# Attention with a gated block behind it: first queries loaded beside the first keys, mixing weights loaded later, and one matmul for the rows that two heads share

## The chip, the cores and the metric

The kernel runs on one core of one Trainium2 chip. The metric is the device time of one execution in microseconds (us), as the median of several runs. A core has TensorE (PE, with weight loads shown apart as PEld), VectorE (DVE), ScalarE (ACT), GpSimd (POOL) and SyncE (SP), which here issues every DMA from one queue.

## The reference

32 heads of attention (4 batches of 8 heads) with 1152 keys of 64 numbers, whose 1152 queries are first averaged in pairs to 576. The 8 heads of a batch are put side by side (512 numbers a row) and go through a gated block with a residual:

```python
q_pool = q.reshape(B, H, S // 2, 2, D).mean(axis=3)       # 576 rows
scores = scale * np.matmul(q_pool, k.transpose(0, 1, 3, 2))
attn = np.exp(scores - np.max(scores, axis=-1, keepdims=True))
attn = attn / (np.sum(attn, axis=-1, keepdims=True) + 1e-09)
x = np.matmul(attn, v)                                    # heads side by side: (4, 576, 512)
h = gelu(x @ w_in)                                        # 1024 wide
u, v = h[..., :512], h[..., 512:]
v_n = layer_norm(v) * g_ln
v_s = np.einsum('ts,bsd->btd', w_sg, v_n) + b_sg[None, :, None]   # the mixing weights w_sg
out = x + (u * v_s) @ w_out
```

## The kernel before, in words

**Work.** The heads go in 16 pairs. Numbers are split in a high and a low 16-bit half so that 16-bit matmuls lose nothing that matters. For a pair, `load` fetches keys (`kr`), queries (`qr`, and the last 128 query rows of each head in `qe`) and values (`vr`, or `va` for two pairs that keep their exponentials in 32 bits). `prepare` finds a scale (a square-sum on ACT, line 393; a matmul with ones, L396; three small DVE operations, L400 to L405), adds the query pairs on POOL (`qs`, L423 and L425), splits keys (ACT L428, DVE L431) and queries (ACT L441, DVE L445) and turns them with DMA transposes into `k1` (L435) and `q1` (L449); L438 copies the high halves of the keys into `k2`, whose other rows are zeroed by POOL once (L905, L906).

**Row maxima.** `maxima` multiplies nine blocks of 128 query rows with the keys (L499) and takes the largest entry of each row by a DVE reduction (L505). Of a head's 576 pooled rows, 512 make four blocks; the last 64 rows of both heads share the ninth block. In the kernel before, these shared rows stand in `q1` twice, as block 4 with only head 0's rows filled and as block 5 with only head 1's, and the maxima of the shared block are two matmuls that add up in one bank. DVE makes the block maxima one number a row (`nm`, L529), POOL splits it and writes it beside the queries (`n2`, L535 to L537), and a transpose (L540) makes `q2`, so that the second of two score matmuls subtracts the maximum.

**Attention.** `unit_of` takes 128 keys at a time: two score matmuls (L574) into a bank `s`, the exponential on ACT (L582), its high half on ACT (L588), its low half by subtraction (L593) and the matmuls with the values (L602; L609 for the two 32-bit pairs) into `avp`. `KEEP` says for which share of the units the exponential stays in the bank and DVE subtracts; for the others it goes to memory and POOL subtracts. At a head's end ACT copies `avp` out (L641), DVE inverts the sums (L644, L645), POOL scales (L648).

**Gated block.** `project` and `gmlp` run once a batch, their matmuls (L757, L857) put between those of the next batch's heads; the last batch has none after it. `weights` loads and splits `w_in` and `w_out`; `spatial` loads `w_sg` (L1058, L1061), finds its scale (L1070 to L1083), turns it on PE (L1110, L1112) and splits it (ACT L1121, DVE L1125). Nothing of `weights` starts before `spatial` is done ("sgdone").

**Order.** Every operation is added to a planner, `Schedule`, with an engine, a cost, what it reads and writes, and a due time. The planner fixes the order on each engine; `PASSES` and the table `MOVES` shift due times before the last pass. Each engine and the SP queue then run in that fixed order and wait in place. L920 adds 40 matmuls with ones that only keep PE busy at the start.

Of the kernel before, what the change touches and what calls it, by code (L numbers as in the profile page):

```python
# [222 lines left out]
def attention_gmlp_kernel(  # L223
# [57 lines left out]
    q2 = tiles(const, 2, [128, 10, 128], F16, "q2")  # L281
    mp = tiles(const, 2, [128, 9, 3], F32, "mp")
    qs = const.tile([128, 10, D], F32, name="qs")
    n1 = const.tile([128, 10, 2, D], F16, name="n1")
    n2 = const.tile([128, 10, 128], F16, name="n2")
# [87 lines left out]
    def scales(p, i, due):  # L373
# [36 lines left out]
        add("DVE", 0.64, power, r=[f"ps{p}{i}"], w=[st, f"pm{i}"], due=due, rel=[("x", "sc", p, i)])  # L410

    def prepare(p):
# [5 lines left out]
        for h in range(2):  # L418
            blk = slice(5 * h, 5 * h + 5)

            def pool(h=h):

                nc.gpsimd.tensor_tensor(out=qs[:, 6 * h:6 * h + 4, :], in0=qr[:, h, :, 0, :], in1=qr[:, h, :, 1, :], op=ALU.add)  # L423
                r = slice(64 * h, 64 * h + 64)
                nc.gpsimd.tensor_tensor(out=qs[r, 4 + h, :], in0=qe[r, 0, :], in1=qe[r, 1, :], op=ALU.add)  # L425
# [14 lines left out]
            def q_hi(blk=blk):  # L440
                nc.scalar.activation(out=n1[:, blk], in_=qs[:, blk].rearrange("p (i t) d -> p i t d", t=1).to_broadcast(  # L441
                    [128, 5, 2, D]), func=AF.Copy, scale=s[:, 1:2])
# [5 lines left out]
            def q_turn(blk=blk):  # L448
                nc.sync.dma_start_transpose(out=q1[c][:, blk], in_=n1[:, blk].rearrange("p i t d -> p (i t d)"))  # L449

            add("POOL", 0.97, pool, r=["qr"], w=[f"qs{h}"], due=t + lead("PL", p) + h)
            add("ACT", 0.72, q_hi, r=[f"qs{h}", sct], w=[f"n1{h}"], due=t + lead("QH", p) + h * HS[p > 0])
            add("SP", 0.7, q_turn, late=LATE[1] * (p > 0), issue=1.25, r=[f"n1{h}"], w=[f"q1{c}{h}"], due=t + lead("QH", p) + h * HS[p > 0])
# [4 lines left out]
            add("DVE", 0.46, q_lo, port=True, r=[f"qs{h}", sct, f"n1{h}"], w=[f"n2q{h}"], due=t + lead("QL", p) + h * HS[p > 0])  # L458
# [22 lines left out]
    def maxima(p):  # L481
# [5 lines left out]
        def rows(r):  # L487

            return ([(0, 4), (1, 5)], [0, 1]) if r == 4 else ([(0, r)], [0]) if r < 4 else ([(1, r + 1)], [1])

        def piece_of(group, j0, nj, g):
            nonlocal n
            r0, x = group[0][0], ("x", p, group[0][0], g)
            w = 128 * nj

            def piece():
                for i, (_, ops, _) in enumerate(group):
                    for k, (h, o) in enumerate(ops):
                        nc.tensor.matmul(out=bank(x)[:, w * i:w * i + w], lhsT=q1[c][:, o, :],  # L499
                                         rhs=k1[c][:, h, j0:j0 + nj, :].rearrange("p j k -> p (j k)"), start=(k == 0),  # L500
                                         stop=(k == len(ops) - 1))

            def top():
# [6 lines left out]
            cols = w * sum(len(ops) for _, ops, _ in group)  # L510
            heads = sorted({h for _, _, hs in group for h in hs})
            add("PE", cols / 2400.0 + 0.003 * len(group), piece, r=[f"q1{c}{h}" for h in heads] + [f"k1{c}{h}" for h in heads], w=[x],
                due=due, acq=(x, where))
            add("DVE", w * len(group) / 960.0 + 0.07, top, r=[x], w=[f"mp{c}{a}{g}" for a, _, _ in group], due=due - 0.5, rel=[x])

        for r in range(9):
            ops, hs = rows(r)

            for g in range(2):
                piece_of([(r, ops, hs)], 4 * g, 4, g)  # L520
            if r in (3, 4, 8):
                piece_of([(a, *rows(a)) for a in {3: range(4), 4: (4,), 8: range(5, 9)}[r]], 8, 1, 2)
            if r in (4, 8):
                due = t + lead("X", p) + lead("XS", p) * n * 1.29 if p else -20 + n
                h = r // 8
                nm = nmx[h]

                def done(h=h, nm=nm):
# [725 lines left out]
```

## Time and profile before

| | before |
|---|---|
| median of 3 runs | 638.8 us (638.28 to 639.22) |
| the profiled execution | 635.98 us, of which its span is 634.2 us |
| PE busy | 603.6 us, 95% of the span |
| DVE, ACT, POOL busy | 528.5, 531.0, 380.8 us |
| DMA packets' time on the SP queue | 51.7% of 16 engines' span |

The profiled execution is 2.8 us below the median. The span runs from the first instruction to the last. Busy times of matmuls overlap, since a matmul's record lasts longer than the distance to the next one.

### The profile page before, as it was taken

The numbers are of one execution on the slowest core, as the hardware profiler recorded it, in microseconds if no ns is written. First come the engines' busy times: TensorE is split into PE (matmuls) and PEld (weight loads), VectorE is DVE, ScalarE is ACT, GpSimd is POOL, SyncE is SP. The second block draws the span as 40 slices with busy tenths as digits, with TensorE's granted clock in tenths as the row PEclk, the third lists the DMA queues.
The fourth block names the chain that finished last, engine by engine and source line by source line (L and its number), as shares of the span: only waits on it lengthen the run. The fifth ranks groups of instructions, "written<-read, shape, count | busy, mean of one in ns | idle before, by whom it ended". The sixth has DMA issues, their size and how long they took to land.

```text
span 634.2 us, 18243 instructions
## 1 busy us (share of the span) xinstructions
PE 603.6 (95%) x7228; PEld 409.2 (65%) x7228; DVE 528.5 (83%) x1052; ACT 531.0 (84%) x987; POOL 380.8 (60%) x481
## 2 busy tenths in 40 slices
PE   5899899997999899999999999999999999999997
PEld 3387567864567566667566775676666775776755
DVE  4989899898989999999987999879998997753662
ACT  7478898799999989999999999798999988784420
POOL 8133375477556688855574677785475565962163
PEclk9999999999999999999999999999999999999999
DMA  9988961957655245568678334807772221141002
GB/s 262 236 209 217 185 135 39 198 121 121 129 115 121 61 79 133 111 136 177 114 160 181 35 51 94 154 24 193 132 170 52 68 41 20 12 84 36 26 1 74
DMA packets 129078, 71.49 MB, mean 113 GB/s; under 512 B 107424, under 2 KB 111520, under 8 KB 128864
## 3 DMA queue, kind: packets, MB, share of 16 engines
q1 hardware_dynamic: 128992, 70.33, 51.7%
q8 instruction: 56, 0.92, 0.6%
q14 instruction: 30, 0.25, 0.1%
HBM read 36.23 MB, written 4.72 MB: 65 GB/s over the span
## 4 chain that ended last, share of the span: by engine, by line
PE 64%; DVE 14%; ACT 5%; issue 1%; DMA 1%; POOL 0%; ACTq 0%; DVEq 0%; POOLq 0%
PE px L757 18%; PE s L574 14%; PE avp L602 13%; PE pm L757 7%; PE px L499 7%; DVE mp L505 5%; DVE f L593 2%; PE s L757 1%; ACT f L588 1%; PE avp L609 1%; ACT e L582 1%; DMA x<-in_moe_w_out_dram 1%; DVE n L445 1%; PE pm L857 1%; DVE dn L644 1%
## 5 line engine op out<-in xcount | busy, mean ns | idle before, releaser
L593 POOL TENSOR_TENSOR f<-e,f 128x512 f16<-128x512 f32 (+2 forms) x182 | 193.0, 1068 | 108.1 <-ACT f L588 93.0
L574 PE MATMUL s<-q,k 128*128 128x512 f16 (+1 forms) x1152 | 231.2, 286 | 12.8 <-ACT e L582 5.2
L505 DVE TENSOR_REDUCE mp<-px 128x1 f32<-128x512 f32 (+2 forms) x316 | 199.8, 663 | 18.1 <-PE px L499 16.2
L602 PEld LDWEIGHTS <-f 128*128 128x128 f16 x3780 | 150.4, 97 | 56.3 <-issue 10.6
L602 PE MATMUL avp<-va,f 128*128 128x65 f16 x3780 | 166.0, 193 | 1.5 <-POOL f L593 1.0
L582 ACT ACTIVATE e<-s 128x512 f32<-128x512 f32 (+2 forms) x226 | 124.9, 558 | 15.6 <-PE s L574 11.1
L499 PE MATMUL px<-k,q 128*128 128x512 f16 (+1 forms) x454 | 118.7, 325 | 2.1 <-DVE mp L505 1.6
L574 PEld LDWEIGHTS <-k 128*128 128x128 f16 x1152 | 82.6, 99 | 51.0 <-issue 15.6
L588 ACT ACTIVATE f<-e 128x512 f16<-128x512 f32 (+2 forms) x182 | 107.1, 591 | 4.5 <-issue 2.0
L593 DVE TENSOR_TENSOR f<-s,f 128x512 f16<-128x512 f32 x126 | 85.9, 682 | 22.7 <-ACT f L588 22.3
L582 ACT ACTIVATE s<-s 128x512 f32<-128x512 f32 x126 | 76.9, 611 | 8.1 <-PE s L574 7.5
L588 ACT ACTIVATE f<-s 128x512 f16<-128x512 f32 x126 | 77.4, 614 | 4.3 <-PE avp L602 2.4
L499 PEld LDWEIGHTS <-q 128*128 128x128 f16 x480 | 42.2, 99 | 27.0 <-issue 6.2
L609 PEld LDWEIGHTS avp<-va,e 128*128 128x128 f32 x360 | 46.1, 192 | 3.1
L609 PE MATMUL avp<-va,e 128*128 128x65 f32 x360 | 45.6, 270 | 0.0
L757 PE MATMUL px<-wsg,vz 128*128 128x512 f16 x168 | 43.6, 379 | 0.0
L423 POOL TENSOR_TENSOR qs<-qr 128x256 f32<-128x256 f32 x32 | 25.1, 786 | 22.3 <-DVE n L445 11.2
L757 PE MATMUL px<-wout_h,xg 128*128 128x512 f32 x100 | 38.2, 425 | 0.0
L757 PEld LDWEIGHTS <-win_h 128*128 128x128 f16 x320 | 30.0, 98 | 12.6 <-issue 1.0
L648 POOL TENSOR_TENSOR x<-a,dn 128x320 f32<-128x320 f32 x32 | 25.3, 789 | 17.2 <-DVE dn L645 13.2
L757 PE MATMUL px<-xt,win_h 128*128 128x288 f16 (+2 forms) x220 | 34.9, 262 | 0.0
L757 PEld LDWEIGHTS <-vz 128*128 128x128 f16 x224 | 20.5, 98 | 20.6 <-issue 0.4
(166 smaller groups left out, 1012.3 us busy)
## 6 DMA issues: line engine op xcount, KB each, us to landing
kr<-in_k_dram SPq DMA_DIRECT2D x16, 576.0 KB, 4.6
qr<-in_q_dram SPq DMA_DIRECT2D x16, 512.0 KB, 4.0
vr<-in_v_dram SPq DMA_DIRECT2D x14, 576.0 KB, 4.1
k<-k SPq DMA_DIRECT2D x32, 144.0 KB, 3.1
x<-in_moe_w_in_dram SPq DMA_DIRECT2D x8, 512.0 KB, 5.9
out_dram<-t SPq DMA_DIRECT2D x16, 256.0 KB, 2.3
x<-in_moe_w_out_dram SPq DMA_DIRECT2D x8, 256.0 KB, 3.5
u<-in_moe_w_sg_dram SPq DMA_DIRECT2D x1, 1152.0 KB, 7.0
```

What stands on the lines that cost most here:

```text
L423: nc.gpsimd.tensor_tensor(out=qs[:, 6 * h:6 * h + 4, :], in0=qr[:, h, :, 0, :], in1=qr[:, h, :, 1, :], op=ALU.add)
L445: nc.vector.scalar_tensor_tensor(out=n2[:, blk, 0:D], in0=qs[:, blk], scalar=s[:, 1:2], in1=n1[:, blk, 0, :], op0=ALU.mult, op1=ALU.subtract)
L499: nc.tensor.matmul(out=bank(x)[:, w * i:w * i + w], lhsT=q1[c][:, o, :], rhs=k1[c][:, h, j0:j0 + nj, :].rearrange("p j k -> p (j k)"), sta ...
L505: nc.vector.tensor_reduce(out=mp[c][:, r0:r0 + len(group), g], in_=src, axis=AX.X, op=ALU.max)
L574: nc.tensor.matmul(out=buf(("s", u))[:, col:col + w], lhsT=kk[c][:, hh, j, :], rhs=qq[:, o:o + w], start=(i == 0 and m == 0), stop=(i == 1 ...
L582: nc.scalar.activation(out=s if kept else buf(("e", u))[:, 0:n], in_=s, func=AF.Exp, scale=SCALE * 2.0**-ASH)
L588: nc.scalar.activation(out=buf(("f", u))[:, 0, 0:n], in_=exponentials(), func=AF.Copy)
L593: eng.tensor_tensor(out=f[:, 1, 0:n], in0=exponentials(), in1=f[:, 0, 0:n], op=ALU.subtract)
L602: nc.tensor.matmul(out=avp[:, o:o + m], lhsT=w[:, col:col + 128], rhs=vv, start=(j == 0 and k == 0 and not tail and x == 0), stop=(j == KJ ...
L609: nc.tensor.matmul(out=avp[:, o:o + D + 1], lhsT=e[:, col:col + 128], rhs=vw[c][:, KJ * hh + j, :], start=(j == 0 and k == 0 and not tail) ...
L648: nc.gpsimd.tensor_tensor(out=xbuf[b % 2][:, :, col], in0=a[:, :, 0:D], in1=d.rearrange("p (i o) -> p i o", o=1).to_broadcast([128, 5, D]) ...
L757: nc.tensor.matmul(out=bank(m)[:, o[0] if o else slice(0, cols)], lhsT=l, rhs=r, start=(k + j == 0), stop=(k + j == n - 1), skip_group_che ...
```

## The change

- The load of the first pair's queries is put right behind that of its keys (`D_LQ`); the load of the mixing weights may not start before the planner's 13 us (`R_S`, 0.16 before), and their turning on PE now waits for their scale.
- The zero rows of the first `k2` are written by DVE; POOL zeroes one block of `n1` where it zeroed all of `qs`.
- The shared rows stand in `n1` once, as block 4 with both heads' rows; POOL copies them crosswise into block 9 (`q_cross`: head 0's rows in the first half of the columns, head 1's in the second). Two copies on the SP queue put the high halves of both heads' keys under each other in `kx`, which there is one of (`k_cross`). The maxima of the shared rows are then one matmul where there were two, with the high halves of the keys alone. They are finished with the second head's rows, so that the first `nm` needs four blocks and not five.
- `KEEP` goes from 0.5 to 0.53. In the last batch the first three units of `project` keep off the score banks, and the others wait for the last head's rows; all units of `project` wait for the scales of `w_in`.
- `PASSES`, `MOVES` (69 entries for 76) and several of the planner's costs are other ones, so the order differs on every engine.

```diff
-    q2 = tiles(const, 2, [128, 10, 128], F16, "q2")
+    q2 = tiles(const, 2, [128, 9, 128], F16, "q2")
+    kx = const.tile([128, KJ, 128], F16, name="kx")
...
+            def q_cross():
+
+                for a in range(2):
+                    r = slice(64 * a, 64 * a + 64)
+                    nc.gpsimd.tensor_copy(n1[r, 9, a, :], n1[r, 4, a, :])
+
+            def k_cross(h=h):
+                nc.sync.dma_start(out=kx[64 * h:64 * h + 64], in_=k1[c][0:64, h])
...
+            if h:
+                add("POOL", 0.45, q_cross, r=["n11"], w=["n1x"], due=t + lead("QH", p) + h * HS[p > 0])
...
+            add("SP", 0.41, k_cross, late=LATE[1] * (p > 0), r=[f"k1{c}{h}"], w=[f"kx{h}"], due=t + lead("KC", p) + h * HS[p > 0])
...
-            return ([(0, 4), (1, 5)], [0, 1]) if r == 4 else ([(0, r)], [0]) if r < 4 else ([(1, r + 1)], [1])
+            if r == 4:
+                return q1[c][:, 9, :], kx, [f"q1{c}1", "kx0", "kx1"]
+            return q1[c][:, r, :], k1[c][:, r // 4 if r < 4 else 1], [f"q1{c}{r // 5}", f"k1{c}{r // 5}"]
...
-        add("POOL", 0.57, lambda: nc.gpsimd.memset(qs, 0.0), w=["qs0", "qs1"], due=-99)
+        add("POOL", 0.2, lambda: nc.gpsimd.memset(n1[:, 9], 0.0), w=["n1x"], due=-99)
...
-        add("POOL", 4.0, lambda: zero_k2(0, nc.gpsimd), w=["k2z0"], due=-15, start=R_Z)
+        add("DVE", 2.3, lambda: zero_k2(0, nc.vector), w=["k2z0"], due=-90)
...
-            add("PE", 0.46, turn, r=["sraw", "srawt", "ident"], w=[x], due=dd, acq=(x, ["X", "M"]))
+            add("PE", 0.46, turn, r=["sraw", "srawt", "ident", "wsc"], w=[x], due=dd, acq=(x, ["X", "M"]))
...
-KEEP = (0.5, 0.5)
+KEEP = (0.53, 0.53)
...
-R_K, R_Q, R_V, R_S, R_Z = 0.0, 21.94, (11.42, 9.34), 0.16, 0.0
+R_K, R_Q, R_V, R_S, R_Z = 0.0, 21.94, (11.42, 9.34), 13.0, 0.0
```

On the SP queue the program begins, before the change, with these DMAs (`u`, `x_89` and `graw` are the mixing weights and their bias and gain; `q_77` and `k_73` are the first pair's `q1` and `k1`, `k_75` its `k2`):

```order
L338 DMA kr<-in_k_dram 128x2x576
L1058 DMA u<-in_moe_w_sg_dram 128x2304
L1061 DMA x_89<-in_moe_w_sg_dram 64x576
L1062 DMA x_89<-in_moe_b_sg_dram 128x576
L1063 DMA graw<-in_moe_g_ln_dram 128x4x1
L341 DMA qr<-in_q_dram 128x2x512
L344 DMA qe<-in_q_dram 64x128 x2
L348 DMA vr<-in_v_dram 128x2x576
L435 DMA_TRANSPOSE k_73<-kn 128x9x128
L352 DMA va_86<-in_v_dram 128x9x64 x2
L449 DMA_TRANSPOSE q_77<-n_84 128x5x128
```

With the change the same place reads (lines are those of the changed kernel: L342 and L345 load queries, L460 turns them, L446 turns keys, L436 makes `kx`, L553 makes `q2`):

```order
L339 DMA kr<-in_k_dram 128x2x576
L342 DMA qr<-in_q_dram 128x2x512
L345 DMA qe<-in_q_dram 64x128 x2
L460 DMA_TRANSPOSE q_77<-n_85 128x4x128
L446 DMA_TRANSPOSE k_73<-kn 128x9x128 x2
L460 DMA_TRANSPOSE q_77<-n_85 128x6x128
L1076 DMA u<-in_moe_w_sg_dram 128x2304
L1079 DMA x_90<-in_moe_w_sg_dram 64x576
L1080 DMA x_90<-in_moe_b_sg_dram 128x576
L1081 DMA graw<-in_moe_g_ln_dram 128x4x1
L349 DMA vr<-in_v_dram 128x2x576
L339 DMA kr<-in_k_dram 128x2x576
```

The queries moved ahead of five loads, all four transposes of the first pair ahead of the mixing weights and of the values. Behind these rows stand the two copies into `kx`, two loads of values and one copy into `k2`, and then the first transpose into `q2`.

On DVE, from the first row maximum on, the order before is 12 reductions (L505) and three small operations up to the first `nm`; the rows at the end of that stretch and behind it are:

```order
L505 TENSOR_REDUCE mp0_81<-px2_145 128x1
L505 TENSOR_REDUCE mp0_81<-px1_144 128x1
L400 TENSOR_SCALAR pm0_105<-pm0_146 128x1
L402 TENSOR_SCALAR sc1_108<-pm0_105 128x1
L405 TENSOR_SCALAR sc1_108<-pm0_105 128x1
L529 TENSOR_REDUCE nm0_115<-mp0_81 128x5
```

With the change (reductions are L520, `nm` is L542) 10 reductions and nothing else stand ahead of it:

```order
L520 TENSOR_REDUCE mp0_82<-px2_146 128x4
L520 TENSOR_REDUCE mp0_82<-pm0_147 128x1
L542 TENSOR_REDUCE nm0_116<-mp0_82 128x4
L520 TENSOR_REDUCE mp0_82<-px0_144 128x1
L520 TENSOR_REDUCE mp0_82<-px2_146 128x1
L520 TENSOR_REDUCE mp0_82<-px1_145 128x1
```

The first `nm` moved forward by two reductions and three small operations. The eleven DVE operations on the mixing weights (five small ones for the scale, six of L1125) stood ahead of the first reduction; now the scale's come six rows behind `nm` and the six others between and behind the last reductions of the pair.

## Rows read from the trace of the kernel before

**Rows 1.** The page's busy time of each engine (share of the span, instructions).

```profile
PE 603.6 (95%) x7228; PEld 409.2 (65%) x7228; DVE 528.5 (83%) x1052; ACT 531.0 (84%) x987; POOL 380.8 (60%) x481
```

**Rows 2.** Five stages: window, length, busy PE, PEld, DVE, ACT, POOL, clock, DMA.

```profile
0.00:20.00 20.00, 11.44 (x59) 6.62 (x60) 10.48 (x28) 15.39 (x24) 13.33 (x23) 1.00 0.95 259
20.00:100.00 80.00, 73.55 (x767) 52.70 (x766) 74.19 (x151) 62.18 (x121) 36.04 (x53) 1.00 0.86 186
100.00:400.00 300.00, 289.14 (x3709) 195.74 (x3708) 276.15 (x554) 284.27 (x536) 197.24 (x251) 1.00 0.56 116
400.00:580.00 180.00, 179.39 (x2368) 120.73 (x2367) 141.26 (x273) 156.59 (x294) 115.79 (x140) 1.00 0.39 81
580.00:634.20 54.20, 50.13 (x332) 33.46 (x330) 26.41 (x50) 12.58 (x14) 18.44 (x17) 1.00 0.13 40
```

**Rows 3.** Timeline of the start: start, length, engine, what, [idle time before].

```profile
4.69 1.16 ACT L393 ACTIVATE kn<-kr 128x1152 bf16<-128x1152 f32 x1 [2.18 <-DMA kr<-in_k_dram]
...
8.26 2.12 ACT L1070 ACTIVATE vz<-u 128x2304 bf16<-128x2304 f32 x1 [0.19 <-DMA u<-in_moe_w_sg_dram]
...
9.62 2.01 POOL L906 MEMSET k<- 3x2304 f16 x1
...
12.04 0.73 POOL L423 TENSOR_TENSOR qs<-qr 128x256 f32<-128x256 f32 x1 [0.42 <-DMA qr<-in_q_dram]
...
13.08 0.83 ACT L441 ACTIVATE n<-qs,sc 128x640 f16<-128x640 f32 x1 [0.17 <-POOL qs L425]
...
15.76 2.06 DVE L1125 SCALAR_TENSOR_TENSOR wsg<-px,wsc,wsg 128x512 f16<-128x512 f32 x3
...
18.36 0.59 PE L499 MATMUL px<-k,q 128*128 128x512 f16 x2
```

**Rows 4.** Timeline from the first maxima to the first scores.

```profile
18.99 1.28 DVE L505 TENSOR_REDUCE mp<-px 128x1 f32<-128x512 f32 x2
...
26.14 0.16 DVE L529 TENSOR_REDUCE nm<-mp 128x5 f32<-128x15 f32 x1
...
27.32 1.21 SPq L540 DMA_TRANSPOSE q<-n  x1
...
27.76 1.24 PE L920 MATMUL avp<-unit_b 128*128 128x512 bf16 x5
...
30.85 0.59 PE L574 MATMUL s<-q,k 128*128 128x512 f16 x2 [0.33 <-POOL qs L423]
```

**Rows 5.** Row maxima by form (count, busy us, mean ns), and one timeline row.

```profile
L499 PE MATMUL px<-k,q 128*128 128x512 f16 x302 | 104.0, 379 | 1.7 <-DVE mp L505 1.3 <-DMA q<-n 0.2
L499 PE MATMUL px<-k,q 128*128 128x128 f16 x152 | 15.5, 219 | 0.4 <-DVE mp L505 0.3
L505 DVE TENSOR_REDUCE mp<-px 128x1 f32<-128x512 f32 x271 | 177.0, 680 | 17.1 <-PE px L499 15.4 <-PE px L396 0.6
21.58 0.38 PE L499 MATMUL px<-k,q 128*128 128x128 f16 x4
```

**Rows 6.** POOL's low halves and two of its small operations, by form.

```profile
L593 POOL TENSOR_TENSOR f<-e,f 128x512 f16<-128x512 f32 x126 | 150.2, 1193 | 88.9 <-ACT f L588 75.9 <-PE s L574 3.3 <-PE px L499 3.2
L425 POOL TENSOR_TENSOR qs<-qe 64x64 f32<-64x64 f32 x32 | 11.4, 357 | 1.3
L536 POOL CAST n<-nm 128x5 f16<-128x5 f32 x32 | 7.6, 239 | 2.2
```

**Rows 7.** DMA issues (count, KB each, median us from issue to landing).

```profile
k<-k SPq DMA_DIRECT2D x32, 144.0 KB, 3.1
k<-kn SPq DMA_TRANSPOSE x32, 4.4
```

**Rows 8.** Timeline: the last values' matmuls, the first result of the last block.

```profile
578.36 0.53 PE L602 MATMUL avp<-va,f 128*128 128x65 f16 x12
...
587.74 0.69 ACT L710 ACTIVATE vz<-s,xs 128x512 f32<-128x512 f32 x1 [6.16 <-PE s L757]
```

**Rows 9.** What PE waited for: total us, times, longest.

```profile
PE s L574 <- ACT e L582: 5.2, 12, 1.2
...
PE s L574 <- DMA q<-n: 2.5, 1, 2.5
```

More of the change, by code (lines that the diff above doesn't have):

```diff
@@ L409, in scales @@
         add("PE", 0.04, spread, r=[f"am{c}{i}", "unit"], w=[f"ps{p}{i}"], due=due, acq=(("x", "sc", p, i), ["X", "M"]))
-        add("DVE", 0.64, power, r=[f"ps{p}{i}"], w=[st, f"pm{i}"], due=due, rel=[("x", "sc", p, i)])
+        add("DVE", 0.26 if i else 0.39, power, r=[f"ps{p}{i}"], w=[st, f"pm{i}"], due=due, rel=[("x", "sc", p, i)])
     def prepare(p):
@@ L509, in piece_of @@
             where = (["X", "M", "S"] if r0 < 4 else ["X", "M"]) if p == 0 else ["X", "M"] if p < NP else XB
[L510 to L514, printed above, removed]
+            cols = w * len(group)
@@ L516, in maxima @@
+            add("PE", cols / 2400.0 + 0.003 * len(group), piece, r=sorted({a for r in group for a in rows(r)[2]}), w=[x], due=due,
+                acq=(x, where))
+            add("DVE", w * len(group) / 960.0 + 0.07, top, r=[x], w=[f"mp{c}{a}{g}" for a in group], due=due - 0.5, rel=[x])
         for r in range(9):
-            ops, hs = rows(r)
             for g in range(2):
-                piece_of([(r, ops, hs)], 4 * g, 4, g)
+                piece_of([r], 4 * g, 4, g)
             if r in (3, 4, 8):
-                piece_of([(a, *rows(a)) for a in {3: range(4), 4: (4,), 8: range(5, 9)}[r]], 8, 1, 2)
@@ L535, in split @@
                     nc.gpsimd.tensor_scalar(out=nm, in0=nm, scalar1=1.0 / MW, scalar2=None, op0=ALU.mult)
                     nc.gpsimd.tensor_copy(hi, nm)
-                    nc.gpsimd.tensor_tensor(out=n2[:, 5 * h:5 * h + 5, D + 1], in0=nm, in1=hi, op=ALU.subtract)
-                def turn(h=h):
-                    nc.sync.dma_start_transpose(out=q2[c][:, 5 * h:5 * h + 5, :], in_=n2[:, 5 * h:5 * h + 5, :].rearrange("p i c -> p (i c)"))
-                add("DVE", 0.17, done, r=[f"mp{c}{a}{g}" for a in range(4 * h, 4 * h + 5) for g in range(3)], w=[f"nm{h}"], due=due - 0.5)
+                    nc.gpsimd.tensor_tensor(out=n2[:, blk, D + 1], in0=nm, in1=hi, op=ALU.subtract)
@@ L543, in maxima, with turn @@
+                def turn(blk=blk):
+                    nc.sync.dma_start_transpose(out=q2[c][:, blk, :], in_=n2[:, blk, :].rearrange("p i c -> p (i c)"))
+                add("DVE", 0.17, done, r=[f"mp{c}{a}{g}" for a in range(blk.start, blk.stop) for g in range(3)], w=[f"nm{h}"], due=due - 0.5)
                 add("POOL", 0.76, split, r=[], w=[f"nm{h}", f"n2m{h}"], due=due - 0.5)
-                add("SP", 0.7, turn, late=LATE[2] * (p > 0), issue=1.25, r=[f"n2q{h}", f"n2m{h}"], w=[f"q2{c}{h}"], due=due - 1)
+                add("SP", 0.7 if h else 0.6, turn, late=LATE[2] * (p > 0), issue=1.25, r=[f"n2q{h}", f"n2m{h}"], w=[f"q2{c}{h}"], due=due - 1)
@@ L696, in project @@
             add("SP", 1.1, x_turn, late=LATE[1] * (b < B - 1), issue=1.3, r=[f"xn{ct % 2}"], w=[f"xt{ct}"], due=dc)
-        ready = [f"xt{ct}" for ct in range(CT if b < B - 1 else CT - 1)]
+        last = b == B - 1
+        ready = ["wn0", "wn1"] + [f"xt{ct}" for ct in range(CT - last)]
+        early = ready + (["nm0", "nm1"] if last else [])
+        if last:
+            ready = ready + [f"x{b % 2}{H - 1}"]
         for i in range(5):
```

67 lines of the change are left out of this document (35 added, 32 removed), and 15 rows, old and new, of the table MOVES.

## The prediction

> **What bounds the kernel now.** I read the page first. PE is busy for 95% of the span; DVE, ACT and POOL have 83%, 84% and 60% [rows 1]. The shares alone do not say that PE is the limit, because a matmul's record lasts longer than the distance to the next matmul. So I read the distance: five matmuls of 512 columns in a row take 1.24 us [rows 4], the record of one is 0.38 us [rows 5], so they start (1.24 - 0.38) / 4 = 0.215 us apart. That is the true price of such a matmul in a full queue.
>
> Then I cut the span into stages [rows 2]. Up to 20 us nothing is full. From 20 to 100 us PE has 73.6 of 80 us and DVE 74.2: both matter. From 100 to 400 us PE has 289 of 300, ACT 284, DVE 276: three engines are near their end together. From 400 us on PE has 179.4 of 180 and then 50 of 54, and the others have room. PE's longest named waits are small: 5.2 us in 12 pieces on the exponentials, and one of 2.5 us on a transpose [rows 9]. So a matmul taken away after 400 us should be worth its full price, one before that a part of it.
>
> The start is a chain of its own [rows 3]. ACT begins on the keys at 4.69 us, when they land. The queries are queued behind the mixing weights, and POOL begins to add them when they land, at 12.04; ACT rounds them at 13.08, a transpose follows, and the first row maxima run at 18.36. From there [rows 4] the reductions begin at 18.99, the first `nm` is made at 26.14, its transpose goes out at 27.32 once POOL has split it, and the score matmuls that need it run at 30.85.
>
> **The change part by part.** *Shared rows.* Per pair there were twice two matmuls of 512 columns and two of 128; half of them go: two of 512 and one of 128. Four of 128 columns take 0.38 us, one record 0.219 [rows 5], so they are (0.38 - 0.219) / 3 = 0.054 us apart. A pair saves 2 x 0.215 + 0.054 = 0.48 us, 16 pairs 7.7 us. The reductions stay as they are: one bank is read for the shared rows before and after. Bounds: 7.7 us if PE is the limit everywhere; if it is so only outside 100 to 400 us, and the 16 pairs lie evenly over the 500 us in which maxima run, 300 / 500 x 7.7 = 4.6 of it are lost and 3.1 left. I take 7.7, and come back to the rest as a rival.
>
> *Queries first.* Mixing weights of 1152 KB landed between 4.69 (keys) and 8.26 us [rows 3], an estimate of 320 KB a us. 576 KB of queries directly behind the keys are then there at 4.69 + 1.8 = 6.5 us. POOL must be free by then: its zeroing of both `k2` ends at 9.62 + 2.01 = 11.6 us, and half of that, two operations of 2.01, goes to DVE, so POOL is free at about 7.6. It adds the first head's queries in 0.73 us (8.3) and ACT rounds them in 0.83 (9.1). A transpose takes SP 1.2 us to issue [rows 4], so the queries go out at 9.1, the keys of head 0 at 10.3. The first maxima need both landed: 10.3 plus between 3.1 (the row of a plain copy) and 4.4 us (a keys' transpose) [rows 7] is 13.4 to 14.7. I take 14.2, 4.2 us ahead of 18.36. DVE gets the zeroing: POOL's price for it was 4.0 us; DVE cannot begin on the keys before ACT has squared them at 4.69 + 1.16 = 5.85 us, and is idle for half of the first 20 us [rows 2], so I cost it nothing; without that cover it would be at most 4 us, on the chain.
>
> *First `nm` from four blocks.* It waits for 10 reductions instead of 12 and three small operations. Two reductions end 1.28 us after the first began and one lasts 0.68 [rows 4, 5], so they are 0.60 apart: 6.0 us instead of 26.14 - 18.99 = 7.15, a gain of 1.1. But on SP 13 DMAs now stand between the last transpose of the pair and the first into `q2`: at 0.5 to 0.6 us each they end at about 14.5 + 8 = 22.5, when `nm` is split at about 22. So I count 0.3 of the 1.1 and put the score matmuls at about 26.3 instead of 30.85: the start is worth 4.5 us. Bounds: 2 us if both of its transposes and the SP queue come a microsecond late, 6 if the SP queue never is.
>
> *What the start costs later.* The mixing weights' turning on PE and splitting on DVE and ACT were done before 18.4 us beside idle engines; now they lie among the maxima. On PE they replace matmuls with ones. On DVE they are six operations (three took 2.06 us [rows 3]) and five small ones, near 5 us, in a stage where DVE is 93% busy [rows 2]. Between nothing and the whole 4.5 us can be lost; I take 2.0, since the splitting of `w_in` in the same stage can wait.
>
> *Low halves.* `KEEP` moves 8 of 252 units from POOL to DVE. On DVE I price one like a reduction over as many numbers, 0.60 us, 4.8 us in all; POOL loses 8 x 1.19 = 9.5 [rows 6]. POOL gets 32 copies of 64 x 64, of which a row of this kernel shows neighbours only: a POOL operation on 128 x 5 at 0.24 us and one on 64 x 64 with two inputs at 0.36. I take 0.3, 9.6 us, about what it loses, on an engine that is idle for 40%; hidden. DVE's 4.8 us fall mostly where it is 92% busy: between nothing and 4.8, I take 2.0.
>
> *Copies into `kx`.* 32 DMAs of the kind `k<-k`, 3.1 us from issue to landing [rows 7], about 0.55 us of SP each. In the order the matmuls on `kx` stand late among a pair's 27, so the landing is covered by the other blocks. Zero, with a rival below.
>
> *The end.* From the last values' matmuls at 578.4 us to the first `vz` at 587.7 [rows 8], while the last head's rows are made, PE works on the last batch's first parts and on the batch before. In the new order about as much of both is left for that place. Zero.
>
> Sum against the profiled execution: 635.98 - 7.7 - 4.5 + 2.0 + 2.0 = 627.8 us. The median of the runs lies 2.8 us above that execution, so 630.6, and I say **630.5 us**.
>
> **Rivals.** *ACT and DVE carry the middle.* From 100 to 400 us ACT is at 95% and does the same work as before; DVE does more. Then the matmuls saved there turn into PE idle time: 4.6 us of the 7.7 are lost, 635.1. For it: the three shares in that stage. Against it: ACT has 180 - 156.6 = 23 us of room from 400 to 580, and the order is a new one, so work can move there. The Trainium skill, page Perfetto Trace Analysis, section Identifying the Most-Contended Engine, says that matmul busy time is a poor measure of PE's headroom and that weight-load busy share and FLOPs should be used; here that share is 65% against ACT's 84%, so by that rule ACT would be the engine to relieve and this rival would hold, at 635.1. The trace agrees that records overlap, and says with the distance of 0.215 us that the queue was nevertheless full after 400 us.
>
> *The start does not pay.* If VectorE is the limit from 20 to 100 us, the 4.5 us are given back in full: 633.1. For it: 74.2 of 80 us. Against it: a good part of that is work that is not due before the first gated block.
>
> *Slower: the new waits.* `kx` is one buffer for two pairs in flight, its copies wait on SP for transposes that landed, and all DMAs behind them wait too; POOL waits in place for ACT before its crosswise copies, with low halves behind it. At 8.3 / 16 = 0.52 us of PE wait a pair the gain is gone; at 0.8, a quarter of one copy's landing, the time is 630.5 + 12.8 = 643. For it: SP's and POOL's queues run in fixed order. Against it: PE waited on a transpose once in the whole run, for 2.5 us [rows 9], and POOL has 40% idle time.
>
> **How the numbers follow.** Forecast 0.55 (its own range 626 to 635), middle carried by others 0.20, start without pay 0.10, slower 0.10, and 0.05 for an order that packs better than 626. A measurement here tells 0.2%, 1.3 us. Faster by more: all of the first, third and last case and three quarters of the second, 0.85; within it 0.06; slower 0.09. The range from 623 to 638 leaves out most of the slower case and the far side of the last.
>
> **What would show it.** First maxima near 14 us and first score matmuls near 26; the maxima's matmuls down by 48; PE still above 97% from 400 us; no wait of PE on `kx` of more than 1 us. The forecast is wrong if PE shows new idle time between 100 and 400 us, if the first head's end is not earlier, or if a wait on SP's queue reaches PE.

## The result, and the profile after

The changed kernel takes 645.99 us (median of 4 runs, 643.54 to 648.64), the kernel before 638.65 (its three runs and one more). The ratio of the runs is 1.0133 with a 95% interval of 1.0105 to 1.0162, so the change makes it slower: by 8.5 us by the ratio, which is used from here on, and by 7.3 us by the two medians alone (1.0115, inside the interval). 630.5 was forecast. In what follows one per cent of the kernel before is 6.4 us, and kernels are compared by their ratio to it.

The page of the profiled execution (647.11 us, span 645.3), its busy times and its clock in 40 slices, against [rows 1]:

```profile
PE 601.7 (93%) x7180; PEld 407.5 (63%) x7180; DVE 534.1 (83%) x1062; ACT 530.6 (82%) x987; POOL 374.4 (58%) x487
...
PEclk9999999999799999999999999999999999999999
```

48 matmuls are gone, as the change says, and the share of every engine but VectorE has gone down: work was taken away and waiting came in. One slice also has a lower granted clock. The stages of [rows 2] (window, length, busy PE, PEld, DVE, ACT, POOL, clock, DMA):

```profile
0.00:20.00 20.00, 11.19 (x38) 4.59 (x39) 13.24 (x27) 5.62 (x8) 9.28 (x22) 0.91 0.62 169
20.00:100.00 80.00, 72.11 (x764) 53.53 (x763) 72.23 (x150) 69.46 (x133) 34.22 (x52) 1.00 1.01 222
100.00:400.00 300.00, 282.00 (x3490) 190.40 (x3488) 263.71 (x532) 267.71 (x504) 193.19 (x245) 0.99 0.54 116
400.00:580.00 180.00, 175.13 (x2399) 118.11 (x2398) 155.92 (x301) 168.21 (x319) 114.77 (x147) 1.00 0.45 96
580.00:645.30 65.30, 61.25 (x500) 40.90 (x498) 29.02 (x56) 19.56 (x28) 22.89 (x22) 1.00 0.12 38
```

From 100 to 400 us all four engines do less than before: 282 against 289 us on PE, 264 against 276 on VectorE, 268 against 284 on ACT, 193 against 197 on POOL. Neither ACT nor VectorE became the bound there.

The last stage is longer by 11 us only because everything before it ends later. The copies of `avp` on ACT (L641, in the changed kernel L655) mark the heads' ends. The eighth head, the last of the first batch, ends at 157.3 us (155.1 before) and the last one at 590.4 (578.9); from there on 54.9 us remain, before 55.3. So the larger part of the loss arises after the first batch and before the last head's end. The two profiled executions are 11.1 us apart, more than the medians, since the one before lies 2.8 us below its median and this one 1.1 above.

What PE waited for, by line and releaser (total us, times, longest), against [rows 9]:

```profile
PE s L588 <- ACT e L596: 7.9, 9, 3.1
PE px L515 <- DVE mp L520: 6.7, 11, 1.5
...
PE px L515 <- DMA k<-kn: 3.0, 2, 2.3
PE s L588 <- DMA q<-n: 2.7, 3, 1.2
PE px L515 <- DMA kx<-k: 2.5, 2, 2.0
```

The start in rows of the timeline (start, length, engine), against [rows 3, 4]:

```profile
13.98 1.05 PE L515 MATMUL px<-k,q 128*128 128x512 f16 x3 [2.29 <-DMA k<-kn]
...
18.71 1.77 SPq L436 DMA_DIRECT2D kx<-k  x2
...
20.38 0.15 DVE L542 TENSOR_REDUCE nm<-mp 128x4 f32<-128x12 f32 x1
...
21.16 2.87 SPq L353 DMA_DIRECT2D va<-in_v_dram  x2
...
24.07 4.36 SPq L449 DMA_DIRECT2D k<-k  x1
28.55 1.24 SPq L553 DMA_TRANSPOSE q<-n  x1
...
28.57 0.38 PE L515 MATMUL px<-kx,q 128*128 128x512 f16 x1 [2.00 <-DMA kx<-k]
...
32.48 0.81 PE L588 MATMUL s<-q,k 128*128 128x512 f16 x3
```

The first maxima run at 13.98 us instead of 18.36 and the first `nm` is made at 20.38 instead of 26.14. Then the lead is lost on SP: the transpose into `q2` goes out at 28.55, later than the 27.32 of before. From 21.16 us on SP is busy in front of it almost without a pause, with two loads of values for 2.87 us and one copy into `k2` for 4.36. The score matmuls that need it run at 32.48, before at 30.85.

Of the other rows, against [rows 6, 7]: low halves and crosswise copies by form, then the copies' issue to landing.

```profile
L607 POOL TENSOR_TENSOR f<-e,f 128x512 f16<-128x512 f32 x118 | 143.4, 1216 | 82.4 <-ACT f L602 60.4 <-PE s L588 5.3 <-DVE f L607 3.3
L607 DVE TENSOR_TENSOR f<-s,f 128x512 f16<-128x512 f32 x134 | 91.1, 681 | 28.1 <-ACT f L602 27.4
...
L433 POOL COPY n<-n 64x64 f16<-64x64 f16 x32 | 10.0, 312 | 10.5 <-ACT n L452 5.6 <-DVE kn L442 3.9
```

```profile
kx<-k SPq DMA_DIRECT2D x32, 144.0 KB, 3.8
k<-k SPq DMA_DIRECT2D x32, 144.0 KB, 4.1
```

The crosswise copies cost POOL 10.0 us (9.6 were counted). The copies into `k2` now take 4.1 us to land instead of 3.1.

My theory at this point was that the work taken away was worth little, and that what was paid is the copies and, above all, that the planner hands out another order on every engine, whose waits fit less well. Rivals: the copies alone; the half clock after idle stretches alone; ACT or VectorE as the bound.

### The profile page after: what moved, and what is told of

It is laid out like the page before. It is cut to its first block, busy times and chain, and to the rows that moved or that the text cites. A ratio compares the mean times of both kernels' runs of the same rounds, so it can differ in the third digit from the quotient of the medians.

```text
span 645.3 us, 18261 instructions
## 1 busy us (share of the span) xinstructions
PE 601.7 (93%) x7180; PEld 407.5 (63%) x7180; DVE 534.1 (83%) x1062; ACT 530.6 (82%) x987; POOL 374.4 (58%) x487
## 5 line engine op out<-in xcount | busy, mean ns | idle before, releaser
L588 PE MATMUL s<-q,k 128*128 128x64 f16 (+1 forms) x1152 | 227.8, 286 | 17.3 <-ACT e L596 7.9
L607 POOL TENSOR_TENSOR f<-e,f 128x512 f16<-128x512 f32 (+2 forms) x174 | 185.8, 1074 | 99.9 <-ACT f L602 75.5
L520 DVE TENSOR_REDUCE mp<-px 128x1 f32<-128x512 f32 (+2 forms) x315 | 198.3, 661 | 18.5 <-PE px L515 16.3
L596 ACT ACTIVATE e<-s 128x512 f32<-128x512 f32 (+2 forms) x218 | 119.2, 549 | 19.1 <-PE s L588 17.4
L607 DVE TENSOR_TENSOR f<-s,f 128x512 f16<-128x512 f32 x134 | 91.1, 681 | 28.1 <-ACT f L602 27.4
L515 PE MATMUL px<-k,q 128*128 128x512 f16 (+1 forms) x361 | 98.4, 329 | 9.4 <-DVE mp L520 5.2
L602 ACT ACTIVATE f<-e 128x512 f16<-128x512 f32 (+2 forms) x174 | 100.8, 582 | 2.3 <-PE avp L616 1.0
L596 ACT ACTIVATE s<-s 128x512 f32<-128x512 f32 x134 | 81.0, 605 | 4.6 <-PE s L588 4.1
L602 ACT ACTIVATE f<-s 128x512 f16<-128x512 f32 x134 | 81.4, 607 | 3.9 <-PE avp L616 1.8
L775 PEld LDWEIGHTS <-xt 128*128 128x128 f16 x224 | 20.8, 98 | 23.5 <-issue 1.6
L775 PE MATMUL px<-win_h,xt 128*128 128x512 f16 x96 | 33.9, 379 | 0.0
```

The source lines that it names most:

```text
L515: nc.tensor.matmul(out=bank(x)[:, w * i:w * i + w], lhsT=qb, rhs=kb[:, j0:j0 + nj, :].rearrange("p j k -> p (j k)"), start=True, stop=True)
L520: nc.vector.tensor_reduce(out=mp[c][:, r0:r0 + len(group), g], in_=src, axis=AX.X, op=ALU.max)
L588: nc.tensor.matmul(out=buf(("s", u))[:, col:col + w], lhsT=kk[c][:, hh, j, :], rhs=qq[:, o:o + w], start=(i == 0 and m == 0), stop=(i == 1 ...
L596: nc.scalar.activation(out=s if kept else buf(("e", u))[:, 0:n], in_=s, func=AF.Exp, scale=SCALE * 2.0**-ASH)
L602: nc.scalar.activation(out=buf(("f", u))[:, 0, 0:n], in_=exponentials(), func=AF.Copy)
L607: eng.tensor_tensor(out=f[:, 1, 0:n], in0=exponentials(), in1=f[:, 0, 0:n], op=ALU.subtract)
```

## The experiments

Ratios to the kernel before, with 95% intervals (the us of work in a name are as counted from the rows):

| kernel | ratio | interval |
|---|---|---|
| changed kernel | 1.0133 | 1.0105 to 1.0162 |
| e1 before, one product | 0.9979 | 0.9961 to 0.9997 |
| e12 before, VectorE -8.5 us | 1.0024 | 0.9999 to 1.0049 |
| e13 before, ACT -7.5 us | 0.9994 | 0.9974 to 1.0015 |
| e14 before, all three cuts | 0.9968 | 0.9939 to 0.9996 |
| e6 before, redrawn | 1.0143 | 1.0117 to 1.0169 |
| e9 before, other list | 1.0120 | 1.0082 to 1.0157 |
| e10 after, other list | 1.0347 | 1.0316 to 1.0378 |
| e7 shared rows alone, new list | 1.0284 | 1.0204 to 1.0363 |
| e8 start alone, new list | 1.0243 | 1.0202 to 1.0284 |
| e2 after, two products | 1.0204 | 1.0173 to 1.0235 |
| e3 after, no copies | 1.0069 | 1.0045 to 1.0092 |
| e16 after, copies by ACT | 1.0328 | 1.0298 to 1.0357 |
| e5 after, late queries | 1.0157 | 1.0132 to 1.0183 |
| e4 after, clock kept at the start | 1.0146 | 1.0115 to 1.0176 |
| e17 after, clock kept at both places | 1.0133 | 1.0111 to 1.0155 |
| e11 before, copies twice to one place | 1.0528 | 1.0472 to 1.0583 |
| e15 before, copies apart | 1.0115 | 1.0087 to 1.0143 |
| e18 the same, wait filled | 1.0079 | 1.0051 to 1.0106 |

Where an operation's work is changed but not its entry in the planner, every engine keeps its order; these are the experiments with "its own order".

**What are the matmuls worth? (e1)**

```diff
-                    for k, (h, o) in enumerate(ops):
+                    for k, (h, o) in enumerate(ops[:1]):
```

> The kernel before with its own order on every engine, instruction by instruction; of the two products of each shared block only the first is made (48 matmuls fewer; the second head's part of the maxima of the shared rows is left out). Nothing else of the change is in it: no copies, no new start, no new order. PE limits everywhere: 638.65 - 7.7 = 631 us. ACT and VectorE carry the middle: 638.65 - 3.1 = 635.5 us. If it is 636 or more, the matmuls removed are worth little in any order; if it is near 631, the term of 7.7 was right and what the changed kernel lost came with the rest of the change.

Measured: 0.21% less, 1.3 us of the 7.7 (0.2 to 2.5 by the interval); the first head ends 0.5 us earlier (49.6), the last one 0.7 (578.2), so hardly anything is gained on the way. One place shows where it can go. The kernel before, PE, where two matmuls of the maxima stand in front of a group of 12 on the values:

```profile
427.16 0.59 PE L499 MATMUL px<-k,q 128*128 128x512 f16 x2
427.59 0.38 PE L574 MATMUL s<-q,k 128*128 128x512 f16 x1
427.81 0.70 PE L602 MATMUL avp<-va,f 128*128 128x65 f16 x12
428.34 0.38 PE L574 MATMUL s<-q,k 128*128 128x512 f16 x1
```

The same place with one of the two left out:

```profile
426.53 0.38 PE L499 MATMUL px<-k,q 128*128 128x512 f16 x1
426.74 0.38 PE L574 MATMUL s<-q,k 128*128 128x512 f16 x1
426.96 0.23 PE L602 MATMUL avp<-va,f 128*128 128x65 f16 x2
427.39 0.48 PE L602 MATMUL avp<-va,f 128*128 128x65 f16 x10 [0.21 <-POOL f L593]
427.70 0.38 PE L574 MATMUL s<-q,k 128*128 128x512 f16 x1
```

From the first matmul to the score matmul at the end it is 428.34 - 427.16 = 1.18 us before and 427.70 - 426.53 = 1.17 after. The 0.21 us saved came back as a wait of 0.21 on POOL's low halves. Before, I read that wait as there too, hidden: the group of 12 took 0.70 us, while the next one, at 428.56, took 0.53.

An estimate from the starts of all matmuls in the traces says the same of the whole run. Take for each shape of matmul the distance to the next start that a quarter of the cases in the kernel before stay under (0.215 us for 512 columns, 0.029 for 65), and call what goes beyond it waiting, at low clock too. Then e1 has 7.8 us less of work, and PE's waiting goes from 49 us in the kernel before to 56 in e1: 7 of the 7.8 us came back as waiting. In the stage from 400 to 580 us the kernel before waits for 6 to 7 us by this estimate, although PE is busy for 99.7% of it and the profile shows 0.6 us of idle time [rows 2]. PE looked full there and still was not what set the time.

**Is another engine the bound? (e12, e13, e14)**

```diff
+                n_r = w // 2 if r0 == 4 and w == 512 else w      # e12, e14: columns that a reduction reads
...
+            w = n // 2 if not tail and g > 30 and int(g) % 7 == 0 else n      # e13, e14: columns that ACT rounds
```

> The kernel before with its own order; the 32 reductions of 512 columns of the shared rows read 256 columns each (half of those maxima is left out), which takes 32 x 0.27 = 8.5 us of work from VectorE and nothing else. VectorE carries the middle: several us, 630 to 634. No single engine carries it, the waits of the order do: 636 to 637.5, like the 7.7 us taken from PE.

> The kernel before with its own order; 35 of the roundings to high halves on ACT, spread over the run, take 256 of 512 columns (the other half of those high halves is left out), 35 x 0.21 = 7.5 us of work from ACT and nothing else. ACT carries the middle: several us, 630 to 634. No single engine carries it: 636 to 637.5.

> The kernel before with its own order and the three cuts together: one product for each shared block (PE -7.7 us), half of the columns in the 32 reductions of the shared rows (VectorE -8.5 us), half of 35 roundings (ACT -7.5 us); the second head's part and half of the shared rows' maxima and half of 35 high halves are left out. The engines are bound jointly: 630 to 633. The waits of the fixed order are the bound (transposes, buffers, the start): 636 to 637.

Measured: taking 8.5 us from VectorE makes nothing faster that can be told (the interval begins at 0.9999), 7.5 us from ACT nothing, and all three cuts together 0.32% or 2.0 us (0.3 to 3.9 by the interval). The cuts are as counted; in the profiled executions VectorE's busy time fell by 4.6 us and ACT's by 6.7. So no one of the three alone is the bound in this order. Engines that bind jointly run side by side, so the three cuts together could give about 7.5 us, the smallest of them, and not their sum of 23.7. They gave about a quarter of it: 634.7 us, with the kernel before at 637.0 beside it, lies between what the joint theory expects (630 to 633) and what the waits of the order expect (636 to 637), and a joint part is left open. POOL was not cut. The Trainium skill, page Perfetto Trace Analysis, section Identifying the Most-Contended Engine, judges PE's headroom by its weight-load share and FLOPs and takes the engine with the highest share first. By the shares of 65% and 84% that was ACT; relieving ACT by 7.5 us gave 0.06% with an interval on both sides of nothing, so the measurement decides against it here.

**What is another order worth? (e6, e9, e10, e7, e8)**

```diff
-PASSES = 14
-MOVES = (...)
+PASSES = 12
+MOVES = ()
```

> The kernel before, with not one operation, transfer, buffer or cost altered: only PASSES is 12 and MOVES is empty, so the planner hands out another order. Loss by the redrawn order: an order that was not picked by moves costs several us, 642 to 646. Loss by the parts of the change alone: an order is an order, 637 to 640.

> The kernel before, with not one operation, transfer, buffer or cost altered, and a longer list of moves: its own 76, then 25 more that each lowered the end that the planner works out for itself, from 625.6 to 621.5. If that end can be trusted: 638 - 4 = 634 us. Loss by the redrawn order: whoever leaves the order at hand pays, however good the planner's own end is: 640 or more.

> The changed kernel, with not one operation, transfer, buffer or cost altered, and a longer list of moves: its own 69, then 75 more that lowered the end that the planner works out for itself from 629.1 to 627.4. Loss by the redrawn order: another draw, anywhere from 640 to 660. The parts of the change carry the loss: within 2 us of 646.

Measured: the very operations of the kernel before take 1.43% and 1.20% longer in two other orders, 9.1 and 7.7 us, as much as the whole change costs; those of the changed kernel 2.1% longer than in its own. The planner's own end, a sum of the costs in its table and no time of the chip, is no guide: an order with 621.5 ran longer than the one with 625.6, and 627.4 longer than 629.1. By the estimate above PE's waiting goes from 49 us to 62 in e6 and 58 in e9 with the same work. In e6 it moved to another place, PE on VectorE's reductions (the kernel before, then e6):

```profile
PE px L499 <- DVE mp L505: 1.6, 5, 0.7
...
PE px L499 <- DVE mp L505: 10.1, 12, 4.8
```

A part of this price goes with PE's granted clock, which is lower in these runs: stretches of low clock hold 11 of the 62 us in e6 and 3 of the 58 in e9, and none of the 49 in the kernel before. Three runs of e9 with a mean clock of 0.993 to 0.995 took 644.0 us on average, and ten of the kernel before with such a clock 639.5, which leaves 4.5 us; for e6's one run at 0.995 (646.5) it leaves 7.0.

The two parts of the change by themselves, each with moves found anew:

```diff
 # e7: the changed kernel with the start and KEEP as before
-D_LQ = (-1900.0, ...
+D_LQ = (2038.8, ...
-KEEP = (0.53, 0.53)
+KEEP = (0.5, 0.5)
-R_S = 13.0
+R_S = 0.16
-        add("DVE", 2.3, lambda: zero_k2(0, nc.vector), w=["k2z0"], due=-90)
+        add("POOL", 4.0, lambda: zero_k2(0, nc.gpsimd), w=["k2z0"], due=-15, start=R_Z)
 # e8: the kernel before with the opposite edits (KEEP is 0.5 already), and the turning of the mixing
 # weights waits for their scale
 # both: another list of moves
```

> The changed kernel without its start (first queries behind the mixing weights, both k2 zeroed by POOL) and with KEEP at 0.5, with a list of moves found anew for it. The shared rows with their copies, the first nm from four blocks and the rest stay. Loss by the redrawn order: with an order picked for it it runs in 632 to 637. Slower through the copies in any order: 640 or more.

> The kernel before with the new start alone (first queries behind the first keys, mixing weights later, first k2 zeroed by VectorE; the weights' turning waits for their scale, without which no order exists), with a list of moves found anew for it. Start worth 4.5 us: 633 to 636. Start paid back among the maxima: 637 to 640. Start harmful: over 640.

Measured: 2.8% and 2.4% longer. Both fall under the last case of what was expected ("640 or more", "over 640"), but they cannot be put down to the copies or the start: in e10 a new list alone cost 2.1%. So they say nothing on the two parts.

**What do the matmuls and the copies weigh in the changed kernel's order? (e2, e3, e16)**

```diff
+                    for _ in range(1 + (r == 4)):      # e2: a shared block's matmul twice
-                nc.sync.dma_start(out=kx[64 * h:64 * h + 64], in_=k1[c][0:64, h])
+                pass      # e3, and POOL's crosswise copies likewise
+                nc.scalar.dma_start(out=kx[64 * h:64 * h + 64], in_=k1[c][0:64, h])      # e16
```

> The changed kernel with its own order; each matmul of a shared block is issued twice, into the same place (48 matmuls more, same result). If PE's work counts in this order too: 646.0 + 7.7 = 653.7 us. If this order has room on PE where the shared blocks stand: 646.0 + 3.1 = 649.1 us or less, down to 646.

> The changed kernel with its own order, without the 32 copies into kx and the 32 crosswise copies on POOL; the shared blocks read the second head's own queries and keys (the first head's part of the maxima of the shared rows is left out). Slower through new waits: the copies cost what is missing, and it runs in 633 to 640 us. Loss by the redrawn order: the copies are beside the point and it stays within 2 us of 646; PE's recorded waits on kx sum to 2.5 us, so 643.5 to 646.

> The changed kernel with its own order, and the 32 copies into kx issued by ACT's queue instead of SP's, at the same places of the program. SP's queue makes them dear: 642 to 643.5. The transfers or the wait for them make them dear: 646. ACT waiting in place for the transposes makes it worse: over 648.

Measured: 7.7 us of matmuls put back cost 0.71%, 4.5 us (about 1.9 to 7.2 by the two intervals). The copies, those on SP and POOL's together, cost 1.0133 - 1.0069, 0.64% or 4.1 us (about 1.7 to 6.4). Both times lie between what the two theories expected. The timeline of e3 shows where about half of the copies' price arises: SP comes to the first `q2` 2.5 us earlier, and the scores that need it run 2.6 us earlier than in the changed kernel.

```profile
26.02 1.23 SPq L553 DMA_TRANSPOSE q<-n  x1
...
29.89 0.81 PE L588 MATMUL s<-q,k 128*128 128x512 f16 x3
```

The second head ends 2.9 us earlier (66.0 instead of 68.9), the last one 5.8. The same copies from ACT's queue (e16) cost 1.95% more, not less. ACT's waits on the keys' transposes, which these copies wait for too, went from 2.7 to 7.9 us; that this is the cause of all of it is not shown.

**What do the copies weigh in the order of before? (e11, e15)**

```diff
                 nc.sync.dma_start(out=k2[c][0:64, h], in_=k1[c][0:64, h])
+                nc.sync.dma_start(out=k2[c][0:64, h], in_=k1[c][0:64, h])        # e11
+                nc.sync.dma_start(out=kx[64 * h:64 * h + 64], in_=k1[c][0:64, h])      # e15
```

> The first experiment again (order of the kernel before, one product for each shared block, the second head's part left out), and with it the price of the crosswise way, as transfers and POOL work alone: each of the 32 copies of keys is issued twice, to the same place, and POOL copies each 64 x 64 piece onto itself ahead of the queries' transpose. If the copies cost what they cost in the changed kernel's order: 636.5 + 4 = 640.5 us. If they are hidden in an order that stays: 636 to 637.

> The first experiment again (order of the kernel before, one product for each shared block, the second head's part left out), with the 32 copies of keys written to a kx of their own that nothing reads, right behind the copies into k2, and POOL's 32 small copies onto themselves; the matmuls with ones go as two of 256 columns, to make room. No copy waits for another. The copies cost what they cost in the changed kernel: 640 to 641. They are hidden where nothing waits for them: 636 to 637. The kernel before had an order without room on SP: over 645.

e11 did not measure what it should: two copies to one place wait for each other. SP's own waits show it (total us, times, longest):

```profile
SPq L439 <- DMA k<-k: 84.8, 32, 5.2
```

That is 2.65 us a copy, and 5.5% of the time against e1: an unplanned wait on SP does reach the end. In e15 no copy waits for another, and they cost, with POOL's small copies, 1.0115 - 0.9979, 1.4% or 8.7 us (about 6.6 to 10.8). In the profiled execution nearly all of it stands at one place of the first pair. PE, and the `q2` transpose that it needs:

```profile
32.64 0.59 PE L577 MATMUL s<-q,k 128*128 128x512 f16 x2 [2.00 <-POOL qs L424]
...
27.45 1.21 SPq L543 DMA_TRANSPOSE q<-n  x1
```

and the windows around it (the last three numbers are the granted clock, the DMA engines' share and GB/s; the last line is the kernel before):

```profile
30.00:32.00 2.00, 0.64 (x4) 0.19 (x2) 2.00 (x4) 0.00 (x0) 0.10 (x1) 1.00 1.29 141
32.00:34.00 2.00, 1.25 (x7) 0.68 (x7) 0.52 (x2) 1.07 (x2) 1.89 (x4) 0.98 0.60 132
34.00:48.00 14.00, 13.71 (x66) 11.52 (x66) 6.95 (x15) 6.39 (x13) 3.66 (x7) 0.50 0.89 183
...
34.00:48.00 14.00, 14.00 (x128) 12.35 (x127) 11.67 (x25) 9.27 (x20) 5.76 (x10) 1.00 0.94 231
```

With two more copies ahead of the `q2` transpose PE idled 2.0 instead of 0.33 us, and then it ran 14 us at half its clock, with 66 matmuls where the kernel before has 128. SP is not what was late here: the transpose went out at 27.45, 0.13 us later than before [rows 4], but took 5.1 us from issue to landing where it took 3.5 before and 3.7 in e1. It landed at 32.60 and the scores began 0.04 us later, as they did behind its landing in the kernel before (30.81) and in e18 (33.86); so I take the 2.00 us as a wait for the landing, though the profile puts them down to POOL's additions. The first head ends 8.5 us later than in the kernel before, the last one 9.4. But the execution with this clock (mean 0.985) took 645.4 us, and three others with 0.993 to 0.997 took 643.5 to 644.2: with less of the half clock the loss is nearly the same.

**Is it the clock? (e4, e17, e18)** In the changed kernel the clock fell twice, each time behind idle PE:

```profile
12.00:14.00 2.00, 0.02 (x1) 0.02 (x1) 0.00 (x0) 0.00 (x0) 0.00 (x0) 1.00 1.12 209
14.00:18.00 4.00, 4.00 (x14) 1.73 (x14) 3.60 (x7) 0.00 (x0) 0.00 (x0) 0.57 0.89 211
158.00:162.00 4.00, 0.59 (x2) 0.19 (x2) 2.99 (x11) 4.00 (x9) 3.48 (x5) 0.90 0.76 170
162.00:168.00 6.00, 5.55 (x54) 3.62 (x54) 5.92 (x13) 6.00 (x12) 2.37 (x3) 0.50 0.92 185
```

```diff
+                for _ in range(6 * first):      # e4, e17: ahead of the first matmul of the maxima
+                    nc.tensor.matmul(out=avp, lhsT=unit_b[:, 0:128], rhs=unit_b, start=True, stop=True)
+            for _ in range({75: 14, 76: 36}.get(u, 0) * (i == 0)):      # e17: ahead of two score matmuls
+                nc.tensor.matmul(out=avp[:, 325:512], lhsT=unit_b[:, 0:128], rhs=unit_b[:, 0:187], ...)
+            for a in range(18 * (u == 0 and i == 1)):      # e18: e15, ahead of the first score matmul with q2
+                nc.tensor.matmul(out=avp[:, 0:256], lhsT=unit_b[:, 0:128], rhs=unit_b, start=True, stop=True)
```

> The changed kernel with its own order and 6 more matmuls with ones ahead of the first matmul of the maxima, where PE idled from 11.8 to 14.0 us before its granted clock fell to a half from 14 to 18 us. If the clock stays at full speed, the first maxima's matmuls run at 0.215 instead of 0.43 us, VectorE's reductions begin at the same time and the time changes by 0 to -2 us: 644 to 646. If the half clock at the start is what cost the gain of the new start, -4 us or more: 642 or less.

> The changed kernel with its own order and matmuls with ones in the three waits of PE ahead of a falling clock: 6 ahead of the first maxima, 14 and 36 of 187 columns (into columns of a bank that nothing reads) ahead of two score matmuls of the ninth head, where PE waited 1.2 and 3.15 us. The clock carries the loss: it stays at full speed and about 10 us at half speed are run at full, 646 - 5 = 641 us. The waits carry it: 644 to 646.

> The order of the kernel before with one product for each shared block and the 32 copies into a place of their own (the second head's part left out), as in the experiment of 644.1 us, and 18 matmuls with ones of 256 columns ahead of the first score matmul with q2, where PE idled for 2.0 us before its clock fell to a half for 14 us. The clock made the copies dear: 637 to 638.5. The copies are dear by themselves: 643 to 644.

Measured: e4 and e17 leave the time where it was (1.0146 and 1.0133). The clock held at the filled places and was low elsewhere; e17:

```profile
12.00:18.00 6.00, 4.45 (x23) 1.94 (x22) 3.45 (x6) 0.00 (x0) 0.00 (x0) 1.00 1.00 217
158.00:164.00 6.00, 5.96 (x78) 5.25 (x78) 4.95 (x17) 6.00 (x12) 3.76 (x6) 1.00 0.80 167
28.00:36.00 8.00, 6.10 (x31) 4.16 (x32) 4.63 (x11) 5.21 (x10) 1.31 (x5) 0.79 1.01 182
164.00:172.00 8.00, 6.00 (x47) 2.96 (x44) 7.97 (x12) 7.99 (x16) 4.43 (x5) 0.79 0.85 173
```

e18's ratio is 0.36% below that of e15, which the two intervals allow to be nothing: the first head ends 5.4 us earlier than in e15, the third one 1.3 and the last one 0.3, because the waits and a low clock (0.57 from 84 to 88 us) came later instead. At the same mean clock the changed kernel is still the slower one: four runs of e17 at 0.996 or 0.997 took 646.9 us on average, 35 of the kernel before with such a clock 637.8. So a low clock enlarges a wait, but it is not what the changed kernel lost most of its time to; a PE that is kept at full clock still waits for the same data.

## Why the prediction was wrong, point by point

**The shared rows, -7.7 us: the step that failed first.** "A matmul taken away after 400 us should be worth its full price" took PE's full queue as proof that PE sets the time. In the order of the kernel before it is worth 1.3 us (e1); in the changed kernel's order the same matmuls added cost 4.5 (e2), and the intervals of the two overlap. The distance of 0.215 us [rows 4, 5] is the price of a matmul where nothing is waited for. I had read two named waits of 5.2 and 2.5 us [rows 9] as all that PE waits for, where the estimate from the starts gives 49 us. Groups that take 0.70 instead of 0.53 us were in the trace; from 400 to 580 us such distances hold 6 to 7 us of waiting, and what was taken away became more of it. In the changed kernel PE waits for 67 us by the same estimate.

**The copies, "zero": failed.** They cost 4.1 us in this order (e3), and 8.7 in the order of before (e15). In the first pair the landing of 3.1 us [rows 7] was not covered: PE waited 2.0 us for `kx` there, and SP had the 13 DMAs in front of `q2` that I had counted myself for another step. Later PE waited for `kx` only once more, for 0.5 us, so the landing was covered as I argued; still about half of what e3 gives back comes after the second head, and which wait that is was not found.

**The start, -4.5 us.** The first half was right: maxima at 13.98 (14.2 forecast), `nm` 5.8 us earlier. The step that failed is "at 0.5 to 0.6 us each they end at about 22.5": SP came to the `q2` transpose at 28.55, and the scores ran at 32.48 instead of the 26.3 forecast, later than before. What is left of it in this order was tried only in part: queries that make the first maxima 1.7 us later (e5) cost 0.24%, 1.5 us, within what the two intervals allow to be nothing.

```diff
+            if p == 0:      # e5, ahead of the first queries
+                nc.sync.dma_start(out=u_t, in_=w_sg[0:TM, :].rearrange("(p i) s -> p i s", i=4))
```

> The changed kernel with its own order, and the 1152 KB of the mixing weights loaded once more, ahead of the first queries (the later load writes the same place again), so that the queries land about 3.6 us later, near where they landed before. If the early start is worth its 4.5 us in this order: 646 + 4 = 650 us. If the start's lead is lost again in the middle: within 1 us of 646.

**What the start costs later, +2.0, and the low halves, +2.0.** Neither was measured by itself. VectorE's low halves went from 126 to 134, as counted; that 8.5 us less on VectorE give nothing in the order of before (e12) says nothing on what more of it costs in this one. This stays open.

**The end, zero: held.** From the last head's end on, 54.9 us remain, before 55.3.

**What the sum had no term for.** It took the new order to be as good as the old one; only "an order that packs better" had a chance, 0.05. The same operations in other orders run 7.7 and 9.1 us longer (e9, e6; 4.5 and 7.0 at the same clock). The parts measured in the changed kernel's own order do not come to its loss: copies 4.1, matmuls between -1.3 and -4.5. Of the 8.5 us (1.33%) that leaves 8.5 - 4.1 + 1.3 = 5.7 to 8.5 - 4.1 + 4.5 = 8.9 for the rest, and that is the size of a redrawn order. That the order is the cause of this rest is the best reading, since e6 shows the size without any part of the change; it is not shown, because the low halves, the later mixing weights and the start came with that order and were not taken apart from it.

**The rivals.** "ACT and DVE carry the middle" was right in that the matmuls were worth little, and wrong in the reason, as far as e12, e13 and the stages after show; e14 leaves it a part. "The start does not pay" came true, with SP busy ahead of `q2` and not with VectorE as the limit. "Slower: the new waits" had the right sign and one of its causes, `kx`, PE's wait of 2.0 us at 28.57; it was given 0.10 because SP's and POOL's reserves were judged by the whole run and not in the first 35 us.

**The signs.** Of what was to show a wrong forecast, new idle time of PE between 100 and 400 us came (282 instead of 289 us busy), and a wait on SP's queue reached PE (2.0 us on `kx`, where none of more than 1 us was to be). The first head ends 0.7 us earlier, as it should, but the second one 0.8 later than before (68.9 instead of 68.1).

No kernel here beats the kernel before and computes all of it; e1 and e14, which ran in 0.998 and 0.997 of its time, leave work out.

## What to carry to other kernels

In this kernel, where several engines run in a fixed order near their end, neither busy shares nor a price list told what an operation is worth. In such a case take it out with the order held (do less inside one operation) and time that first, before changing what the planner sees. If the change forces a new order, give the sum a term for the order, as wide as the spread of a few redrawn orders of the unchanged kernel. Look for new transfers first in the pair that nothing covers, and count what stands ahead of them on their queue by the rows of that stretch.

## What the hardware showed that I had not expected

The granted clock of PE went to half (1.2 of 2.4 GHz) behind some idle stretches and not behind others as long. After 2.29 us it stood at 0.57 for 4 us in the changed kernel, and after 2.00 us at 0.50 for 14 us in e15. In e1 PE idled 2.27 us up to 77.78, and the clock stood at 0.51 from 78.5 to 82; the kernel before idled 2.46 us at the same place, up to 78.47 [rows 9], and stayed at 1.00, as the changed kernel did behind the 2.00 us up to 28.57. What decides between them is not shown. Runs of one and the same kernel, the one before, go with their mean granted clock: 17 runs at 1.000 lie at 636.1 us on average, 10 at 0.993 to 0.995 at 639.5.

The issue of a transfer on SP held SP for 4.36 us in the changed kernel (the copy at 24.07), and the same copy at 31.64 for 0.60. The DMA engines' share was 1.18 in the first stretch and 0.72 in the second, but the kernel before issued its first such copy, at 19.12, in 0.54 us at a share of 1.17, so that share alone does not tell; what held SP was not found.
